# Block-sparse attention and two dense layers on one core: later batches' value preparation re-timed, and one pair of value gathers put one step later

## The chip, the cores and the metric

The kernel runs on one core of one Trainium2 chip. TensorE (PE) multiplies, VectorE (DVE), ScalarE (ACT) and GpSimd (POOL) do elementwise work, and SyncE (SP) issues nearly all of the DMAs, in the order in which the program names them. The metric is the device time of one execution in microseconds (us).

## The reference

Four batches, eight heads, 768 positions, 64 values per head. Attention is masked in blocks of 32: a row of blocks sees its own block and its two neighbours, the first and the last block, and three sampled blocks; the first and the last row of blocks see everything. Two dense layers follow.

```
scores = q @ k.T / sqrt(64), masked by blocks
attn   = softmax(scores) @ v                      # (4, 8, 768, 64)
x      = attn as (3072 tokens, 512)
h      = x @ w_in                                  # (3072, 2048)
g      = h * erf(softplus(h))
out    = g @ w_out                                 # (3072, 512)
```

## The kernel before, in words

All products of the two dense layers and of attention with the values are taken as sums of float16 halves.

**Units.** Attention is cut into 16 units per batch, 64 in all, numbered 0 to 63 here. Ten "m" units of a batch cover four rows of blocks and four heads each; four "f" units and two "e" units cover the rest. A unit's work is: scores on PE (`scores`, tile s), maximum on DVE and exponentials on ACT (`soft_max`, `soft_exp`), a split into halves on DVE (`soft_low`, tile p), and a transpose by DMA from the SP queue (`soft_turn`, tile pT). The product with the values (`values_of`, into the tile po_bank) comes three units later, then a normalisation on DVE (`norm`). After every second unit of a group of rows `turn` makes two halves and transposes them by DMA from the SP queue into xT, which the first dense layer reads.

**Steps.** From unit 4 on, the main loop runs 98 steps, 0 to 97. Every step has one group of the first dense layer on PE (24 products into the tile h), its elementwise work on ACT and DVE (tiles x, q, g), and one group of the second layer from two steps ago (tile o). A table (`until`) tells in which steps a unit is added: in every step up to 17, and then in about two steps of three. Step 18, 21 and 23 for instance have none. Step 16 starts with the PE row at 237.33 us, step 24 with that at 293.65 us.

**Order.** Every engine and every DMA queue works strictly in the order in which the program is written; nothing is reordered. So a DMA that waits on the SP queue holds all later ones, and an ACT instruction that waits for a load holds the elementwise work of the next dense group behind it.

**Values.** A batch's values are prepared a batch ahead, by pairs of heads (four pairs). `load_v` loads a pair (SP, 384 KB, tile vraw, a single buffer). `square_v` sums its squares on ACT (tile vj). `scale_v` adds these over partitions with two small PE products into a corner of po_bank and makes a scale on DVE (tile m_v). `high_v` (ACT) and `low_v` (DVE) write the halves into the tile vn. The write of vn into a table in DRAM (vtab) goes out on SP at the start of the next step. `behind(n)` runs at the end of the step of unit n and calls these; `prepare` puts the compute of a part off to the next step. With n the unit's number within its batch, the pair r is loaded at n = 3 + 3r, its squares are prepared one unit later and its scale and halves two units later.

**Gathers.** `gather_v(b, i)` fills two of eight slots of the tile vb from the table of batch b for rows of blocks i and i + 1: on SP, 9 DMAs for a pair whose slots don't yet hold the batch's first and last block and lie side by side, 12 where the two slots are the last and the first, 7 for each later pair. `gathers` decides in each step how many pairs go out: as many as slots are free, within a room of 4 blocks per step; a pair counts double where it is called fresh. A pair's DMAs stand on the SP queue ahead of the step's `soft_turn` and `turn`.

In the second batch (units 16 to 31) the pair i = 1 is gathered in step 12, i = 3 and i = 5 in step 14, i = 7 in step 15; products with the values of units 16, 17 and 18 (which read rows 1 to 4, 1 to 4, and 5 to 8) stand in steps 15, 16 and 17.

Of the kernel before, what the change touches and what calls it, by code (L numbers as in the profile page):

```python
# [43 lines left out]
def sparse_attention_moe(ctx: ExitStack, tc: tile.TileContext, qT, kT, v, sampled, w_in, w_out, out):  # L44
# [23 lines left out]
    B, H, D, S = qT.shape  # L68
# [7 lines left out]
    HP = H // 2  # L76
# [3 lines left out]
    KGS, VGS = 4, 8  # L80
# [35 lines left out]
    def load_k(b, pr):  # L116

        if b == 0:
            if pr < 3:
                kr = at.tile([P, 1024], F32, tag="pT", name=f"kr_{b}_{pr}", bufs=PV_LAG + 1)[:, :S]  # L120
            else:
                kr = at.tile([P, KT * 2 * VW], F16, tag="vn", name=f"kr_{b}_{pr}", bufs=1).bitcast(F32)[:, :S]
        else:
            kr = wi[:, NK * NG :, :].rearrange("p n c -> p (n c)")[:, :S]
        sp.dma_start(kr, kT[b, 2 * pr : 2 * pr + 2].rearrange("t d s -> (t d) s"))
        krs[b, pr] = kr

    def order_k(b, pr):
        kx = key_blocks(b).rearrange("p n (a c) -> p n a c", c=BLOCK)
        kr = krs.pop((b, pr))  # L130
        copy = pool.tensor_copy if b else dve.tensor_copy if pr > 1 else act.copy
        copy(kx[:, :NB, pr, :], kr.rearrange("p (n c) -> p n c", c=BLOCK))
        copy(kx[:, NB, pr, :], kr[:, :BLOCK])
# [4 lines left out]
    def load_q(b, t):  # L138
        place, tag, bufs = (mo, "g", FF_LAG + 1) if b == 0 and t in (1, 2) else (ld, "qt", 2)
        qt = place.tile([P, HP, P], F32, tag=tag, name=f"qt_{b}_{t}", bufs=bufs)  # L140
        rows = qT[b].rearrange("(r t) d s -> (t d) r s", t=2)
        if t < MT:
            c = (1 + 4 * t) * BLOCK
            sp.dma_start(qt, rows[:, :, c : c + P])
        else:
            sp.dma_start(qt[:, :, : 3 * BLOCK], rows[:, :, S - 3 * BLOCK :])
            sp.dma_start(qt[:, :, 3 * BLOCK :], rows[:, :, :BLOCK])
        qts[b, t] = qt
# [5 lines left out]
    def load_v(b, pr):  # L154

        if b == 0:
            vr = vb[:, 2 * pr : 2 * pr + 2].rearrange("p x a c -> p x (a c)").bitcast(F32)[:, :, : KT * D]
        else:
            vr = ld.tile([P, 2, KT * D], F32, tag="vraw", name=f"vraw_{b}_{pr}", bufs=1)
        sp.dma_start(vr, v[b][:, 2 * pr : 2 * pr + 2].rearrange("p h k d -> p h (k d)"))  # L160
        vraws[b, pr] = vr
# [237 lines left out]
    def gather_v(b, first):  # L399

        rows, last = vtab[b], first + 2
        at_ = [next(ring) % VGS for _ in range(first, last)]
        slot_of.update({(b, i): x for i, x in zip(range(first, last), at_)})
        fresh = [x for x in at_ if ended.get(x) != b]
        for x, y, _, _ in runs([(x, x) for x in fresh]):
            for q, n in ((2, 0), (3, NB - 1)):
                ends = rows[n * BLOCK : (n + 1) * BLOCK].unsqueeze(1).to_broadcast([BLOCK, y - x, 2 * QW])
                sp.dma_start(vb[q * BLOCK : (q + 1) * BLOCK, x:y, 1], ends)
        for x in fresh:
            ended[x] = b  # L410
        for x, y, n, m in runs(zip(at_, range(first, last))):
            lo, hi = int(n == 1), 3 - int(m == NB - 1)
            if lo:
                sp.dma_start(vb[:BLOCK, x, 0], rows[NB * BLOCK :])
            if hi < 3:
                sp.dma_start(vb[2 * BLOCK : 3 * BLOCK, y - 1, 0], rows[NB * BLOCK :])
            if y - x == 1 or lo or hi < 3:
                for j in range(y - x):
                    a, e = (lo if j == 0 else 0), (hi if j == y - x - 1 else 3)
                    c = (n + j - 1) * BLOCK  # L420
                    sp.dma_start(vb[a * BLOCK : e * BLOCK, x + j, 0], rows[c + a * BLOCK : c + e * BLOCK])
            else:
                around = rows[(n - 1) * BLOCK : (n + 2) * BLOCK]
                windows = bass.AP(around.tensor, around.offset, [around.ap[0], (BLOCK * 2 * QW, y - x), around.ap[1]])
                sp.dma_start(vb[: 3 * BLOCK, x:y, 0], windows)
        for j, x in enumerate(at_):
            for r, (q, half) in enumerate(PLACES):
                n = block_number(SYNC, first + j, r)
                sp.dma_start(vb[q * BLOCK : (q + 1) * BLOCK, x, half], rows[bass.ds(n * BLOCK, BLOCK), :])

    def whole_v(b, k):

        slot_of[b, -1 - k] = x = next(ring) % VGS
        ended.pop(x, None)
        sp.dma_start(vb[:, x], whole_rows(b)[:, 2 * k : 2 * k + 2])
# [396 lines left out]
    per = len(units) // B  # L832
    have_k, have_v = set(), set()
    kfree, vfree = KGS, VGS

    def gather_keys():

        nonlocal kfree
        if kjobs and kfree >= 4 and kjobs[0][0] in have_k:
            kfree -= 4  # L840
            gather(*kjobs.pop(0))

    def gathers(m):

        nonlocal vfree
        gather_keys()
        room = VGS if begun == 0 else 2 if begun <= NEAR else 4
        while vjobs and vjobs[0][0] in have_v:
            b, i = vjobs[0]
            n = 2 if i > 0 else 1  # L850
            fresh = b > 1 and 0 < i < VGS
            if vfree < n or room < n * (1 + fresh):
                break
            vfree -= n
            room -= n * (1 + fresh)
            vjobs.pop(0)
            gather_v(b, i) if i > 0 else whole_v(b, -1 - i)
# [9 lines left out]
    def behind(m):  # L867

        b, n = divmod(m, per)
        if b + 1 < B:  # L870
            c = b + 1
            if n == 10:
                load_q(c, 0)
            k = n - 4 if b else 2 * (n - 10) if n > 9 else -1
            if k in ((1, 3, 5, 7) if b else (2, 4, 6, 8)):
                order_k(c, (k - 1) // 2)
            if k in (0, 2, 4, 6):
                load_k(c, k // 2)
            if k == 8:
                have_k.add(c)  # L880
            pr, k = divmod(n - 3, 3)
            if pr in range(HP):
                if k == 0:
                    load_v(c, pr)
                if k == 1:
                    prepare((c, pr), None, square_v, None)
                if k == 2:
                    prepare((c, pr), scale_v, high_v, low_v)
                    if pr == HP - 1:
                        prepare((c,), None, None, join_scales)  # L890
            if pr == HP and k == 0:
                have_v.add(c)

    prepared = []

    def prepare(args, *parts):

        prepared.append([part and partial(part, *args) for part in parts])
# [50 lines left out]
    have_k.add(0)  # L949
    hold_blocks(POOL)  # L950
    gathers(0)
    hold_blocks(SYNC)
    for i in range(4, 10):
# [18 lines left out]
    scores(units[1])  # L972
    used_keys(units[1])
    gathers(0)
    for i in range(10, 16):
        load_weight(pool, "i", i)
# [26 lines left out]
    first_scale(0)  # L1003
    values_of(seen(units[1]))
    gathers(0)
    for i in (12, 13, 14, 15):
        load_weight(sp, "o", i)
# [15 lines left out]
    work("Do3 Hi2 Li2 Hi3 Li3")  # L1023
    begun = FIRST
    behind(begun - 1)

    on_pe[0] = False
# [4 lines left out]
    for m in range(len(groups) + FF_LAG):  # L1032
        ch, i = divmod(m, NGR)
# [73 lines left out]
        if unit:  # L1107
            behind(begun - 1)
# [39 lines left out]
```

## Time and profile before

| | us |
|---|---|
| median of 3 runs | 787.42 (784.93 to 789.92) |
| the profiled execution's own time | 787.68 |
| its span, first to last instruction | 785.9 |
| PE busy | 691.7 (88%) |
| DVE busy | 573.9 (73%) |
| ACT busy | 550.3 (70%) |

PE is the busiest engine and, from about 140 us on, it works almost without a break; what it waits for there is lost time. A row of the timeline reads: start, duration, engine, line, operation, what is written and read, how many, and in brackets the engine's idle time just before it with what ended that idle time. SPq rows are DMA issues; their duration is that of issuing, not of the transfer. Line numbers are all L60, a helper's, so the rows are told apart by tiles.

### The profile page before, as it was taken

To read this page: it belongs to the slowest core of one execution; us is meant where nothing else is said; L and a number is where in the kernel's file an instruction comes from. 1 tells how busy PE (TensorE), PEld (TensorE's weight loads), DVE (VectorE), ACT (ScalarE), POOL (GpSimd) and SP (SyncE) were. 2 spreads that over 40 slices of the span, in tenths; PEclk is the share of its full clock that TensorE was granted. 3 is DMA by queue.
4 is the path that set the end of the run, shared out by engine and by line. 5 is a ranking of instruction groups with operands and counts; after the bars stand their busy time and mean duration, and the time that the engine had idled before them with its cause. 6 is when DMAs were issued, how large, how long until landed. Compare 5 with 4: busy or idle time off the path is not lost.

```text
span 785.9 us, 26669 instructions
## 1 busy us (share of the span) xinstructions
PE 691.7 (88%) x10868; PEld 461.8 (59%) x10868; DVE 573.9 (73%) x1025; ACT 550.3 (70%) x943; POOL 123.9 (16%) x340
## 2 busy tenths in 40 slices
PE   2345727899979998999999989999999999999996
PEld 1234524566646665666767656666677666666663
DVE  3897887998876858877678858767778777654543
ACT  4665677998655767877677667777677776766774
POOL 4702121102411112011112111111011110000000
PEclk9999968999999999999999989999999999999999
DMA  8998973789688997974687996935777777410000
GB/s 314 277 304 264 313 168 82 151 194 253 151 185 184 215 200 160 215 148 104 148 192 164 203 203 166 233 81 138 139 151 199 163 160 179 63 42 2 20 23 27
DMA packets 200779, 129.24 MB, mean 164 GB/s; under 512 B 144080, under 2 KB 167760, under 8 KB 200656
## 3 DMA queue, kind: packets, MB, share of 16 engines
q1 hardware_dynamic: 197808, 117.83, 63.6%
q0 software_dynamic: 2848, 9.71, 3.7%
q8 instruction: 85, 1.39, 0.8%
q14 instruction: 38, 0.31, 0.2%
HBM read 81.52 MB, written 12.95 MB: 120 GB/s over the span
## 4 chain that ended last, share of the span: by engine, by line
PE 72%; DVE 12%; ACT 5%; issue 4%; DMA 4%; SPq 1%; POOL 1%; POOLq 0%; ACTq 0%; DVEq 0%
PE o L60 29%; PE h L60 28%; PE po_bank L60 7%; PE s_m L60 6%; DVE keys L60 3%; PE s_f L60 3%; DMA wo<-in_w_out_dram 2%; DVE mx_m L60 2%; DVE p_m L60 1%; ACT pf_m L60 1%; DVE wi L60 1%; DVE g L60 1%; SPq L60 1%; DVE wo L60 1%; ACT x L60 1%
## 5 line engine op out<-in xcount | busy, mean ns | idle before, releaser
L60 PE MATMUL h<-xT,wi 128*128 128x256 f16 x2304 | 272.4, 275 | 9.9 <-DMA xT<-x 4.8
L60 PE MATMUL o<-wo,g 128*128 128x512 f16 x1152 | 271.5, 383 | 4.9 <-ACT wo L60 2.2
L60 PEld LDWEIGHTS <-wi 128*128 128x128 f16 x2304 | 227.2, 99 | 60.3 <-issue 7.3
L60 PEld LDWEIGHTS <-g 128*128 128x128 f16 x1152 | 108.2, 99 | 137.8 <-issue 25.1
L60 ACT ACTIVATE x<-x 128x512 f32<-128x512 f32 x288 | 181.5, 630 | 9.1
L60 POOL COPY keys<-keys 128x128 f32 x264 | 91.2, 394 | 342.1 <-PE s_m L60 297.9
L60 DVE SCALAR_TENSOR_TENSOR q<-x,q 128x512 f32<-128x512 f32 x96 | 68.4, 712 | 68.7 <-ACT x L60 68.7
L60 ACT ACTIVATE x<-h,isg 128x512 f32<-128x512 f32 x96 | 65.8, 685 | 67.7 <-PE h L60 65.8
L60 ACT ACTIVATE pf_m<-s_m,nb_m 128x256 f32<-128x256 f32 x160 | 62.6, 473 | 46.3 <-DVE nb_m L60 43.4
L60 ACT ACTIVATE q<-q 128x512 f32<-128x512 f32 x96 | 60.7, 632 | 30.4 <-DVE q L60 30.4
L60 PE MATMUL s_m<-keys,qt 64*32 64x192 f32 (+1 forms) x1600 | 70.3, 355 | 9.6 <-ACT pf_m L60 7.9
L60 DVE SCALAR_TENSOR_TENSOR q<-q,h 128x512 f32<-128x512 f32 x96 | 65.5, 682 | 17.3 <-ACT q L60 17.3
L60 DVE SCALAR_TENSOR_TENSOR g<-q,g 128x512 f16<-128x512 f32 x96 | 67.0, 698 | 3.3
L60 ACT ACTIVATE q<-x 128x512 f32<-128x512 f32 x96 | 60.5, 630 | 3.1
L60 PEld LDWEIGHTS s_m<-keys,qt 64*32 64x32 f32 (+1 forms) x1600 | 45.9, 135 | 21.4 <-ACT pf_m L60 8.9
L60 PE MATMUL po_bank<-vb,pT_m 128*32 128x65 f16 (+1 forms) x3840 | 43.7, 203 | 13.8 <-DVE m_v L60 4.7
L60 DVE TENSOR_REDUCE mx_m<-s_m 128x4 f32<-128x1024 f32 x40 | 48.8, 1220 | 9.1 <-PE s_m L60 8.8
L60 PEld LDWEIGHTS <-pT_m 128*32 128x32 f16 x3840 | 38.1, 99 | 23.4 <-issue 17.2
L60 DVE TENSOR_TENSOR p_m<-pf_m,p_m 128x1024 f16<-128x1024 f32 x40 | 50.1, 1252 | 1.6 <-ACT p_m L60 0.3
L60 DVE TENSOR_SCALAR g<-q 128x512 f16<-128x512 f32 x96 | 41.3, 430 | 3.3
L60 DVE CAST p_m<-pf_m 128x1024 f16<-128x1024 f32 x30 | 20.9, 697 | 24.5 <-ACT pf_m L60 23.0
L60 POOL COPY keys<-wi 128x768 f32<-128x768 f32 (+1 forms) x24 | 16.7, 723 | 125.0 <-DMA wi<-in_kT_dram 125.0
(111 smaller groups left out, 529.9 us busy)
## 6 DMA issues: line engine op xcount, KB each, us to landing
vb<-vtab SPq DMA_DIRECT2D x280, 65.0 KB, 2.9
vb<-vtab SPq DMA_DIRECT2D x32, 390.0 KB, 4.3
vtab<-vn SPq DMA_DIRECT2D x16, 390.0 KB, 5.0
vb<-vtab SPq DMA_DIRECT2D x12, 520.0 KB, 5.2
qt<-in_qT_dram SPq DMA_DIRECT2D x20, 256.0 KB, 4.0
out_dram<-wo SPq DMA_DIRECT2D x20, 256.0 KB, 2.7
vb<-vtab SPq DMA_DIRECT2D x36, 130.0 KB, 3.3
vraw<-in_v_dram SPq DMA_DIRECT2D x12, 384.0 KB, 4.8
```

Source lines behind the costliest of these rows:

```text
L60: done = call(*args, **kwargs)
```

## The change

Two edits, both in functions that set order alone; no instruction is added or removed, but for where it stands.

The first alters when a pair of the second batch counts double in `gathers`: now its first two pairs (i = 1 and 3) do. Step 14 then takes i = 3 alone, and step 15 takes i = 5 and i = 7. Nothing else of the gathers moves.

The second alters `behind` for the values of the third and fourth batch (batches 2 and 3). Pair r is loaded at unit 4r − 1 of the batch ahead (the first one at the last unit of the batch before that), its squares are prepared two units later, its scale and halves three units later. The first batch's schedule for the second batch's values stays.

```diff
-            fresh = b > 1 and 0 < i < VGS
+            fresh = 0 < i < (0, VGS // 2, VGS, VGS)[b]
...
-            pr, k = divmod(n - 3, 3)
-            if pr in range(HP):
-                if k == 0:
-                    load_v(c, pr)
-                if k == 1:
-                    prepare((c, pr), None, square_v, None)
-                if k == 2:
-                    prepare((c, pr), scale_v, high_v, low_v)
-                    if pr == HP - 1:
-                        prepare((c,), None, None, join_scales)
-            if pr == HP and k == 0:
-                have_v.add(c)
+            if n == per - 1:
+                have_v.add(c)
+        if b == 0 and n < per - 1:
+            c, early = 1, 1
+            pr, k = divmod(n - 3, 3)
+        else:
+            c, early = (m + 1) // per + 1, 0
+            pr, k = divmod((m + 1) % per, 4)
+        if c < B and pr in range(HP):
+            if k == 0:
+                load_v(c, pr)
+            if k == 2 - early:
+                prepare((c, pr), None, square_v, None)
+            if k == 3 - early:
+                prepare((c, pr), scale_v, high_v, low_v)
+                if pr == HP - 1:
+                    prepare((c,), None, None, join_scales)
```

In steps of the main loop this gives, for the third batch's four pairs and then the fourth batch's:

| | before | now |
|---|---|---|
| load (end of step) | 15, 19, 24, 28; 38, 43, 48, 52 | 11, 15, 20, 26; 32, 38, 44, 50 |
| squares on ACT | 17, 21, 26, 30; 41, 45, 50, 54 | 14, 18, 25, 30; 36, 42, 49, 54 |
| scale and halves | 18, 23, 27, 31; 42, 47, 51, 55 | 15, 20, 26, 31; 37, 44, 50, 55 |

Before, all eight of the last line are steps without a unit; now 15, 20, 26, 44 and 50 have one.

SP, from the end of step 11 to step 12, one piece of the difference. vraw_0 is the load of the first pair of the third batch, vtab_95 the second batch's table and vn_3 the write of its last pair, which the gathers vb<-vtab_95 behind it read.

```order
 L60 DMA qt_1_3078<-in_qT_dram 128x4x128
 L60 DMA_TRANSPOSE pT_e_1_3105<-p_e_1_3097 128x8x128
+L60 DMA vraw_0_3113<-in_v_dram 128x768
 L60 DMA vtab_95<-vn_3_3099 128x6x260
 L60 DMA vb<-vtab_95 32x2x1040 x2
```

The load now stands on the queue ahead of the table's last write, and so of all gathers of the second batch.

SP in step 14, one piece of the difference. The first two rows end the pair i = 3, the last two begin the pair i = 5; pT_m_1_0 is unit 18's transpose, xT_2 the one that step 16's first dense layer reads.

```order
 L60 ISA
 L60 DMA vb<-vtab_95 32x1040
+L60 DMA_TRANSPOSE pT_m_1_0_3602<-p_m_1_0_3595 128x16x128
+L60 DMA_TRANSPOSE xT_2_2558<-x_0_5_3604 128x8x128
 L60 DMA vb<-vtab_95 32x2x1040 x2
 L60 DMA vb<-vtab_95 96x2x1040
```

Both transposes now stand 9 DMAs earlier, and the pair i = 5 stands behind them.

ACT around the squares of the third batch's second pair (vj_1), before and then now. x_2_6<-h_2_6 begins the elementwise work of step 22, x_2_3<-h_2_3 that of step 19.

```order
L60 ACTIVATE q_2_5_4751<-q_2_5_4751 128x512
L60 ACTIVATE vj_1_4773,vsq_1_4772<-vraw_1_4517 128x768
L60 ACTIVATE x_2_6_4800<-h_2_6_4775,isg_736 128x512
L60 ACTIVATE x_2_6_4800<-x_2_6_4800 128x512 x2
L60 ACTIVATE q_2_6_4804<-x_2_6_4800 128x512
```

```order
L60 ACTIVATE q_2_2_4291<-q_2_2_4291 128x512
L60 ACTIVATE vj_1_4315,vsq_1_4314<-vraw_1_3844 128x768
L60 ACTIVATE x_2_3_4342<-h_2_3_4317,isg_736 128x512
L60 ACTIVATE x_2_3_4342<-x_2_3_4342 128x512 x2
L60 ACTIVATE q_2_3_4346<-x_2_3_4342 128x512
```

The squares moved from step 21 to step 18; their load moved from the end of step 19 to that of step 15.

## Rows read from the trace of the kernel before

**Rows 1.** The page: memory rate in 40 slices, and a DMA group's landing time.
```profile
GB/s 314 277 304 264 313 168 82 151 194 253 151 185 184 215 200 160 215 148 104 148 192 164 203 203 166 233 81 138 139 151 199 163 160 179 63 42 2 20 23 27
...
vb<-vtab SPq DMA_DIRECT2D x280, 65.0 KB, 2.9
```

**Rows 2.** Timeline of PE, steps 15 to 18.
```profile
227.50 0.90 PE L60 MATMUL po_bank<-vb,pT_m 128*32 128x65 f16 x89 [0.45 <-DMA vb<-vtab]
...
237.33 4.44 PE L60 MATMUL h<-xT,wi 128*128 128x256 f16 x24 [4.83 <-DMA xT<-x]
...
246.59 2.78 PE L60 MATMUL h<-xT,wi 128*128 128x256 f16 x24
249.30 0.96 PE L60 MATMUL po_bank<-vb,pT_m 128*32 128x65 f16 x96
...
254.20 2.78 PE L60 MATMUL h<-xT,wi 128*128 128x256 f16 x24
```

**Rows 3.** Timeline of the SP queue, 202 to 286 us.
```profile
202.22 0.52 SPq L60 DMA_DIRECT2D vtab<-vn  x1
205.87 7.03 SPq L60 DMA_DIRECT2D vb<-vtab  x11
...
214.84 1.17 SPq L60 DMA_DIRECT2D qt<-in_qT_dram  x1
...
235.85 6.42 SPq L60 DMA_DIRECT2D vb<-vtab  x12
...
246.47 0.58 SPq L60 DMA_DIRECT2D vraw<-in_v_dram  x1
...
283.90 1.81 SPq L60 DMA_DIRECT2D vraw<-in_v_dram  x1
```

**Rows 4.** Timeline of the SP queue, the first 9 of step 14's 18 gathers.
```profile
219.92 6.05 SPq L60 DMA_DIRECT2D vb<-vtab  x9
```

**Rows 5.** Timeline of PE, steps 24 and 25, then 48 and 49.
```profile
293.65 2.78 PE L60 MATMUL h<-xT,wi 128*128 128x256 f16 x24
298.85 1.50 PE L60 MATMUL po_bank<-vb,pT_m 128*32 128x65 f16 x96 [2.42 <-DVE m_v L60]
...
305.13 2.78 PE L60 MATMUL h<-xT,wi 128*128 128x256 f16 x24
...
461.24 2.78 PE L60 MATMUL h<-xT,wi 128*128 128x256 f16 x24
466.29 1.50 PE L60 MATMUL po_bank<-vb,pT_m 128*32 128x65 f16 x96 [2.27 <-DVE m_v L60]
...
474.12 2.78 PE L60 MATMUL h<-xT,wi 128*128 128x256 f16 x24
```

**Rows 6.** Timeline of ACT, the second pair's squares of the third and fourth batch.
```profile
288.73 0.84 ACT L60 ACTIVATE vj<-vraw 128x768 bf16<-128x768 f32 x1 [5.71 <-DMA vraw<-in_v_dram]
...
456.18 0.84 ACT L60 ACTIVATE vj<-vraw 128x768 bf16<-128x768 f32 x1 [5.46 <-DMA vraw<-in_v_dram]
```

**Rows 7.** Timeline of DVE: unit 18's split, a pair's low halves, the late scale.
```profile
225.88 1.23 DVE L60 TENSOR_TENSOR p_m<-pf_m,p_m 128x1024 f16<-128x1024 f32 x1
...
262.51 1.15 DVE L60 SCALAR_TENSOR_TENSOR vn<-vraw,vs,vn 128x384 f16<-128x384 f32 x2 [1.20 <-ACT vn L60]
...
298.64 0.15 DVE L60 TENSOR_SCALAR m_v<-po_bank 128x1 f32<-128x1 f32 x1
```

**Rows 8.** The third batch's step 36: SP timeline, and that xT's landing.
```profile
392.93 1.90 SPq L60 DMA_TRANSPOSE pT_m<-p_m  x1
394.92 1.71 SPq L60 DMA_TRANSPOSE xT<-x  x1
...
xT<-x SPq DMA_TRANSPOSE x1, 3.2
```

**Rows 9.** Busy time by stretch (PE, PEld, DVE, ACT, POOL), PE clock, DMA share, GB/s.
```profile
247.00:303.00 56.00, 53.16 (x961) 37.42 (x960) 41.20 (x79) 39.52 (x73) 9.44 (x32) 0.97 0.88 197
...
466.00:473.00 7.00, 6.71 (x143) 3.98 (x143) 5.59 (x16) 4.73 (x9) 2.22 (x6) 0.51 0.93 158
```

## The prediction

> **What bounds the kernel now.** I read the page first: PE is the busiest engine, and from about 140 us on its timeline has hardly a gap. So I looked for the rows of PE with an idle time over 1 us, and asked of each what is late and who issued it. Between 140 and 770 us three are large.
>
> The first is in step 16: the dense product waits 4.83 us for xT, and then takes 4.44 us [rows 2]. The step before had already waited twice for gathers, the last time 0.45 us. The second and third are in steps 24 and 48: the product with the values waits 2.42 and 2.27 us for DVE to read the scale sum (m_v) out of po_bank [rows 5].
>
> What a step costs undisturbed is seen from step 17 to 18: 254.20 − 246.59 = 7.61 us [rows 2]. By this measure step 24 took 305.13 − 293.65 = 11.48, so it lost 3.87 us, and step 48 took 474.12 − 461.24 = 12.88 and lost 5.27 [rows 5]. Step 16 took 246.59 − 237.33 = 9.26, so 1.65 us were lost after its wait, 6.48 with it [rows 2]. That losses exceed waits is the clock: behind the third wait the granted clock is 0.51 of full speed, the 1.2 GHz level [rows 9]. PE has no work that could cover such a loss. The three sum to 6.48 + 3.87 + 5.27 = 15.62 us, 2.0% of the run; that is all that the change can take back.
>
> Why they are late: for xT, the SP queue. The order shows its transpose behind 18 gathers of step 14, of which the first 9 alone take 6.05 us to issue [rows 4]. For m_v, ACT: the squares of the second pair wait 5.71 and 5.46 us for their load [rows 6], which the SP queue issued only at 283.90 for an ACT that was free at 283.0 (288.73 − 5.71) [rows 3, 6]. The elementwise work behind is late by as much, DVE idles, and reads m_v at 298.64 [rows 7] where PE, at 298.85 − 2.42 = 296.43, already wants the bank.
>
> **The change, part by part. Step 16.** The pair i = 5 leaves step 14, so unit 18's transpose may start once its 9 gathers are issued and p is split. The gathers begin at 219.92 and end at 225.97 [rows 4], p is ready at 225.88 + 1.23 = 227.11 [rows 7]. In the third batch the same two transposes follow a lone pair: from the first one's issue to xT's landing it takes 394.92 + 3.2 − 392.93 = 5.19 us, to the end of issue 394.92 + 1.71 − 392.93 = 3.70 [rows 8]. So xT lands at about 232.3, where PE asks for it at 237.33 − 4.83 = 232.50 [rows 2]. The 6.48 go.
>
> Two things are paid back. First, the load that now stands ahead of the table's last write. The write is issued at 202.22 and the gathers wait for it until 205.87 [rows 3]. The load adds its issue, 0.58 [rows 3], and 384 KB ahead on the same queue, at the best rate of the page, 314 GB/s [rows 1], 1.25: together up to 1.83, at least nothing. Some is absorbed: the issue of the queries at 214.84 takes 1.17 [rows 3], mostly waiting. I take 1.1. Step 15 already waits for gathers, so this comes through: its products end 1.1 later, and PE asks for xT at 233.6.
>
> Second, the pair i = 5 is now late itself, with i = 7 behind it, and unit 18's product with the values in step 17 wants both. SP begins them at 227.15 + 3.70 = 230.85; 9 DMAs as in step 14 take 6.05 [rows 4], the 12 of i = 7 6.42 [rows 3], so the last is issued at 243.3 and lands 2.9 later [rows 1], at 246.2. PE comes there at 233.6 + 7.61 + (249.30 − 246.59 = 2.71) = 243.9 [rows 2], and waits 2.3 us. That is the length of the waits of 2.42 and 2.27 that lost the clock [rows 5], not of 0.45, after which the step ran on [rows 2], so I add the 1.65 of step 16. Net: the product starts at 246.2 instead of 249.30 [rows 2], 3.1 gained, less 1.65: **1.5 us**. Bounds: with the gathers 2 us slower and the loss of clock of step 48 (5.27 − 2.27 = 3.0), 3.1 − 2 − 3.0 = −1.9; with no load to wait for and no return in step 17 at all, 6.5. The order's own rows say most for the low half, since the same number of DMAs must pass the queue before step 17.
>
> The Trainium skill (DMA: Bandwidth & Descriptors, Anatomy of one DMA — SWDGE path) puts a DMA at about 2.0 us plus bytes over 436 GB/s, an estimate of 2.15 us for these 65 KB, for the software path. By it the wait in step 17 would be 0.75 shorter and the gain of this part 2.3; here the median is 2.9 [rows 1], and I go by that.
>
> **Steps 24 and 48.** The second pair's load moves from the end of step 19 to that of step 15, from 283.90 to where the first pair's load stood, about 246.47 [rows 3], and its squares from step 21 to 18. Step 18 starts at 254.20 [rows 2], 1.5 earlier now, and the squares follow its exponentials, so ACT comes to them more than 6 us after the load is issued instead of just before it. The wait of 5.7 us goes, DVE's idle with it, and step 23 has no scale any more. What is late next there: nothing within 2 us that I see on PE's timeline, since PE runs without a gap on both sides. I take back **3.87 us** in full, and in the fourth batch, with the same table, **5.27**. Bounds for each: nothing, if the new place meets another wait, to full.
>
> **What moves besides.** The four pairs of two batches keep their instructions: squares, halves and scales are the same number. Their cost on ACT and DVE is covered by idle time, 56.00 − 41.20 = 14.8 us of DVE in 247 to 303 alone [rows 9]. The table writes go out one step behind the halves as before, and the halves of a batch's last pair stay in their step, so no gather of batches 2 and 3 has its table later. In step 32 the early load stands ahead of gathers that are needed five steps later. I take nothing.
>
> **Sum.** 1.5 + 3.9 + 5.3 = 10.6 us off the profiled execution's 787.68: **777.1 us**, 1.3% faster. The median of the runs is 0.26 lower than that execution, so the sum holds against it too.
>
> **Rivals.** (1) *The forecast*: 773.5 to 780. Chance 0.60.
>
> (2) *No return*: the gathers of step 15 land in time, because the queue is less crowded than in step 14. The whole 15.6 comes back: 772.0. For it: DMAs are issued sooner overall. Against: SP's rows show no free stretch there. 0.12.
>
> (3) *The DMA engines are the bound*. In 247 to 303 their share is 0.88 [rows 9], 49 of 56 us. If what PE gains only lets transfers queue longer, the first part gives nothing and step 24's wait turns into one for gathers: only 5.3 is left, 782.4. For it: the same bytes in less time. Against: 56 − 49 = 7 us are free, more than 3.9. The Trainium skill (Trainium Kernel Development and Optimization, Key Constraints) states that all issuing queues share the same 16 DMA engines, so that moving an issue buys no bandwidth; no row here contradicts it, and this rival is what it would do. 0.15.
>
> (4) *The load waits anyway*. vraw is one buffer; the next load must wait for the halves of the pair before, which now lie in the same step as the load. If the squares still find no data, steps 24 and 48 stay: 786.2. Against: SP issued step 19's load at 283.90 [rows 3], less than two steps before step 24 at 293.65 [rows 5], so halves of the load's own step are long done when SP comes to it. 0.08.
>
> (5) *Slower*. Scale and halves now lie in steps 15, 20, 26, 44 and 50, which have a unit. Each puts 4 × 0.15 + 1.15 us on DVE and 1.20 of waiting for ACT [rows 7], 2.95. If DVE has no slack in a step with a unit, normalisation is late, po_bank stays taken, and PE waits 2.95 and loses 1.65 of clock in each: 5 × 4.6 = 23, so 777.1 + 23 = 800.1. It decides where DVE's delay outlasts the step. Against: four of the five are followed by a step without a unit, in which DVE has its maximum, split and normalisation less. 0.05.
>
> **Range and chances.** Two in ten left out: below 771.5 and above 783.5; that takes in (2), (3) and nearly all of (1). A change of under 1%, 7.9 us, is what a measurement of this kernel hardly tells from none, so faster means below 779.5. Of (1) 0.55 lies there, (2) wholly, of (3) 0.03: faster 0.70. Slower is (5), 0.05; the rest, 0.25, is within 1%.
>
> **What would show it.** PE's row of step 16 should have no wait on xT, and step 17's product a wait of 1 to 4 us on vb<-vtab; no wait there means (2), over 4 us with a larger loss means the first part is negative. ACT's vj rows should have no idle on vraw, and steps 24 and 48 no wait on m_v; a vj row that still waits for vraw is (4), a wait on vb or pT in steps 20 to 26 is (3). Waits of PE on rinv or xf in steps 16, 21, 27, 45, 51 are (5). I am wrong in the main if steps 24 and 48 keep their loss under another name.

## The result and the profile after

The changed kernel takes **778.66 us** (median of 6 runs, 776.68 to 783.39), beside 788.12 (784.93 to 789.92, 6 runs) for the kernel before on the same chip: a ratio of **0.9889, interval 0.9853 to 0.9926**. It is faster by 1.1%. The forecast was 777.1. The profiled execution took 780.28, its span 778.5.

A step is timed below from the first row of its first dense layer (h<-xT,wi) to that of the next step, as in the prediction, so a wait ahead of that first row counts in the step before. The three steps that the sum was made of, and the other steps that moved by over 1 us (us):

| step | 12 | 14 | 15 | 16 | 17 | 24 | 41 | 48 |
|---|---|---|---|---|---|---|---|---|
| before | 6.72 | 10.03 | 14.17 | 9.26 | 7.61 | 11.48 | 7.74 | 12.88 |
| after | 7.97 | 11.19 | 10.17 | 7.60 | 12.19 | 7.61 | 9.05 | 7.61 |

Step 12 does not belong to the change: its dense product starts at 200.34, ahead of the first instruction that moved (the load issued at 202.27, below), and takes 4.03 us instead of 2.78, at a granted clock of 0.50 of full speed from 200 to 202, the 1.2 GHz level. None of the other profiled runs shows that there.

By stretch, the 7.4 us between the two spans lie so: −0.1 (a loss) up to step 10, −1.0 in steps 11 to 19, 3.6 in steps 20 to 35, 4.2 in steps 36 to 59, 0.7 behind.

**Steps 24 and 48 are undisturbed.** The timeline of PE in the changed kernel (start, duration, then the idle time before a row in brackets, where there is any), steps 24 and 48 with the start of the next:

```profile
295.09 2.78 PE L60 MATMUL h<-xT,wi 128*128 128x256 f16 x24
297.80 0.96 PE L60 MATMUL po_bank<-vb,pT_m 128*32 128x65 f16 x96
...
302.69 2.78 PE L60 MATMUL h<-xT,wi 128*128 128x256 f16 x24
...
459.97 2.78 PE L60 MATMUL h<-xT,wi 128*128 128x256 f16 x24
462.68 0.96 PE L60 MATMUL po_bank<-vb,pT_m 128*32 128x65 f16 x96
...
467.58 2.78 PE L60 MATMUL h<-xT,wi 128*128 128x256 f16 x24
```

No product waits for m_v any more, which answers to [rows 5]. The reason stands in ACT's timeline, the squares of the third batch's second pair and the fourth batch's first and second:

```profile
263.63 0.83 ACT L60 ACTIVATE vj<-vraw 128x768 bf16<-128x768 f32 x1
...
388.82 0.86 ACT L60 ACTIVATE vj<-vraw 128x768 bf16<-128x768 f32 x1
...
428.73 0.83 ACT L60 ACTIVATE vj<-vraw 128x768 bf16<-128x768 f32 x1
```

None has an idle time on vraw, where [rows 6] showed 5.71 and 5.46 us. The load of the first of these three is issued at 251.87 (below), 11.8 us ahead of its use.

**Steps 15 to 17: the wait has moved.** PE's timeline from the products of step 15 on:

```profile
229.51 0.20 PE L60 MATMUL po_bank<-vb,pT_m 128*32 128x65 f16 x1 [0.37 <-DMA vb<-vtab]
230.10 1.37 PE L60 MATMUL po_bank<-vb,pT_m 128*32 128x65 f16 x93 [0.39 <-DMA vb<-vtab]
...
236.39 2.78 PE L60 MATMUL h<-xT,wi 128*128 128x256 f16 x24 [0.68 <-DMA xT<-x]
...
...
244.00 2.78 PE L60 MATMUL h<-xT,wi 128*128 128x256 f16 x24
246.71 0.56 PE L60 MATMUL po_bank<-vb,pT_m 128*32 128x65 f16 x3
248.58 0.31 PE L60 MATMUL po_bank<-vb,pT_m 128*32 128x65 f16 x4 [1.32 <-DMA vb<-vtab]
249.79 0.90 PE L60 MATMUL po_bank<-vb,pT_m 128*32 128x65 f16 x89 [0.90 <-DMA vb<-vtab]
250.62 2.56 PE L60 MATMUL s_m<-keys,qt 64*128 64x64 f32 x40
...
256.18 2.78 PE L60 MATMUL h<-xT,wi 128*128 128x256 f16 x24
```

The wait for xT is 0.68 instead of 4.83 us [rows 2], and step 16 takes an undisturbed 7.60. In step 17 the product with the values now waits 1.32 + 0.90 = 2.22 us for gathers, and what follows runs slow: s_m takes 2.56 where it takes 1.47 elsewhere. The busy time by stretch (PE, PEld, DVE, ACT, POOL, granted clock, DMA share, GB/s) shows why:

```profile
250.00:254.00 4.00, 4.00 (x131) 2.50 (x115) 1.39 (x4) 0.15 (x1) 0.70 (x3) 0.58 1.02 210
```

The granted clock is 0.58 of full speed, so mostly the 1.2 GHz level, right behind the two waits.

The SP queue's timeline, which answers to [rows 3, 4]:

```profile
202.27 0.53 SPq L60 DMA_DIRECT2D vraw<-in_v_dram  x1
202.89 0.39 SPq L60 DMA_DIRECT2D vtab<-vn  x1
207.66 6.95 SPq L60 DMA_DIRECT2D vb<-vtab  x11
...
221.29 7.43 SPq L60 DMA_DIRECT2D vb<-vtab  x9
230.19 1.81 SPq L60 DMA_TRANSPOSE pT_m<-p_m  x1
232.09 2.21 SPq L60 DMA_TRANSPOSE xT<-x  x1
234.40 13.87 SPq L60 DMA_DIRECT2D vb<-vtab  x21
...
251.87 0.53 SPq L60 DMA_DIRECT2D vraw<-in_v_dram  x1
```

The 9 and 12 gathers of i = 5 and i = 7 now go out in one run of 21. They take 13.87 us, 0.66 each in the mean (19 of the issues take 0.32 to 0.53 us, two 1.24 and 2.02, and register instructions between them the rest), and the last is issued by 248.27; PE's last wait in step 17 ends at 249.79.

### The profile page after: what moved, and what is told of

Read it like the earlier page. It is cut to its first block, busy times and chain, and to the rows that moved or that the text cites. A ratio compares the mean times of both kernels' runs of the same rounds, so it can differ in the third digit from the quotient of the medians.

```text
span 778.5 us, 26676 instructions
## 1 busy us (share of the span) xinstructions
PE 688.5 (88%) x10868; PEld 459.6 (59%) x10868; DVE 573.6 (74%) x1025; ACT 551.5 (71%) x943; POOL 120.0 (15%) x340
## 4 chain that ended last, share of the span: by engine, by line
PE 66%; DVE 14%; ACT 6%; DMA 6%; issue 4%; SPq 2%; POOL 0%; POOLq 0%; ACTq 0%; DVEq 0%
PE o L60 26%; PE h L60 25%; PE po_bank L60 6%; PE s_m L60 5%; DVE keys L60 4%; PE s_f L60 3%; SPq L60 2%; ACT x L60 2%; DMA pT_m<-p_m 2%; DVE p_m L60 2%; DMA vb<-vtab 2%; DVE wo L60 1%; ACT pf_m L60 1%; DVE mx_m L60 1%; DVE wi L60 1%
## 5 line engine op out<-in xcount | busy, mean ns | idle before, releaser
L60 POOL COPY keys<-keys 128x128 f32 x264 | 88.6, 383 | 325.3 <-PE s_m L60 283.0
L60 PE MATMUL s_m<-keys,qt 64*32 64x192 f32 (+1 forms) x1600 | 68.1, 347 | 9.3 <-ACT pf_m L60 6.4
```

What stands on the lines that cost most here:

```text
L60: done = call(*args, **kwargs)
```

## The experiments

All times below are medians beside the kernel before on the same chip, with the ratio to it and its 95% interval. The sums of steps 11 to 19 and 20 to 35 are from the profiled runs; before they are 78.41 and 111.86, after 79.45 and 108.25.

**1. Which of the two edits gains.** The gathers alone (`behind` as before):

```diff
-            fresh = b > 1 and 0 < i < VGS
+            fresh = 0 < i < (0, VGS // 2, VGS, VGS)[b]
```

> The gather edit alone; the values' schedule as in the kernel before. Theory A (the gain is all in the values; the gathers' wait only moves): step 16 loses its wait of 4.8 us on xT, step 17 gains one of 2 to 3 us on vb with a loss of clock, in sum 0 to 2 us gained; steps 24 and 48 lose 3.9 and 5.3 as before; 786 to 788 us. Theory B (the gathers are what gained, because the SP queue's whole delay in the second batch begins there): step 24's wait on m_v goes too, since its load is issued earlier; 780 to 783 us.

Measured: 791.31 beside 790.35; **1.0015 (0.9988 to 1.0042)**. By step 20 it is 3.35 us ahead (75.06 instead of 78.41), and steps 20 to 35 take 4.85 more (116.71). That is nearest to theory A, though steps 24 and 48 lose more than before. The timelines of SP, ACT and PE show where it goes; first SP:

```profile
284.99 0.43 SPq L60 DMA_DIRECT2D vraw<-in_v_dram  x1
```

Then ACT, the squares of the second pair, and PE in step 24:

```profile
289.94 0.84 ACT L60 ACTIVATE vj<-vraw 128x768 bf16<-128x768 f32 x1 [10.20 <-DMA vraw<-in_v_dram]
```

```profile
300.05 1.51 PE L60 MATMUL po_bank<-vb,pT_m 128*32 128x65 f16 x96 [4.80 <-DVE m_v L60]
```

The load goes out at 284.99, no sooner than before (283.90, [rows 3]), though PE is ahead. ACT waits 10.20 for it instead of 5.71, PE 4.80 for m_v instead of 2.42. Step 23 takes 7.32 instead of 5.35 and step 24 14.25 instead of 11.48, 4.74 of the 4.85 us. What the gathers gain is lost again at the late load.

The values alone (`fresh` as before, `behind` changed):

> The values' edit alone; gathers as in the kernel before. Theory A: the waits of steps 24 and 48 go (9.1 us), step 41 waits about 1.3 us more, and the load ahead of the table's write in step 12 makes steps 12 to 16 later by about 1.5 us, with step 16's wait on xT still there at 4 to 6 us; 779 to 782 us. Theory B: little, at most the 5.3 us of step 48; 783 to 787 us.

Measured: 779.83 (778.04 to 782.53); **0.9865 (0.9829 to 0.9900)**, no less gain than the whole change. Steps 24 and 48 take 7.60 and 7.61. Step 16 keeps its wait, on PE's timeline:

```profile
240.65 4.19 PE L60 MATMUL h<-xT,wi 128*128 128x256 f16 x24 [4.66 <-DMA xT<-x]
```

So the gain is that of the values, and the gathers add nothing that these runs could show (0.9889 and 0.9865, with intervals that overlap). No version that was tried and computes everything is shown to be faster than these two.

**2. Is it the lateness of one load?** In the kernel before, only the second pair's load is moved, by one step:

```diff
-                if k == 0:
+                if k == 0 and (c < 2 or pr != 1):
                     load_v(c, pr)
...
                     if pr == HP - 1:
                         prepare((c,), None, None, join_scales)
+                    if c > 1 and pr == 0:
+                        load_v(c, 1)
```

> The kernel before, with one thing moved in the third and the fourth batch: the load of the second pair of values is issued one step sooner (end of steps 18 and 42 instead of 19 and 43); squares, scales, halves and all else stay in their steps. Theory A (steps 24 and 48 lose because this load is late for the squares in steps 21 and 45): the squares find their data, steps 24 and 48 take 7.6 to 9 us instead of 11.48 and 12.88, and 5 to 9 us of the whole come back: profiled 779 to 783. Theory B (they lose because the work of a pair falls on too few steps, squares, scale and halves one after the other): m_v is still read late, steps 24 and 48 stay over 11 us, 786 to 789. The load must wait for the first pair's halves, which are made in the same step, and holds the gathers behind it on SP: a wait on vb in step 19 or 20 of up to 3 us would take back a part of A's gain.

Measured: 782.42 beside 789.11; **0.9917 (0.9881 to 0.9953)**. On its timelines SP issues the load at 270.14 instead of 283.90, ACT squares it without a wait, and step 24 has no wait on PE:

```profile
270.14 0.53 SPq L60 DMA_DIRECT2D vraw<-in_v_dram  x1
...
273.28 11.16 SPq L60 DMA_DIRECT2D vb<-vtab  x15
```

```profile
285.26 0.83 ACT L60 ACTIVATE vj<-vraw 128x768 bf16<-128x768 f32 x1
```

```profile
295.97 2.78 PE L60 MATMUL h<-xT,wi 128*128 128x256 f16 x24
298.69 0.96 PE L60 MATMUL po_bank<-vb,pT_m 128*32 128x65 f16 x96
...
303.57 2.78 PE L60 MATMUL h<-xT,wi 128*128 128x256 f16 x24
```

Steps 24 and 48 take 7.60 and 7.61, with squares, scales and halves where they were. It is the load's lateness that cost 3.87 and 5.27 us. Step 20 takes 1.25 more (8.86), part of what was expected for holding the gathers.

**3. The load ahead of the table's write.** The third batch's first load moved behind step 12's gathers:

```diff
-            if k == 0:
+            if k == ((c, pr) == (2, 0)):
                 load_v(c, pr)
```

> Both edits, but the third batch's first load at the end of step 12 instead of step 11, so behind the second batch's last table write and the first gathers. If that load costs what stands ahead of it in the changed kernel, gathers of step 12 begin about 1.8 us earlier after the write, step 14's products of scores and step 15's wait on vb shrink by about 1 us each, step 17's wait shrinks little because the load now stands ahead of step 14's transposes; 1 to 2 us below the changed kernel. If the queue's total before step 17 is all that counts, the same time within 0.7 us.

Measured: 783.35 (778.59 to 784.15); **0.9892 (0.9853 to 0.9931)**, as the changed kernel; the 1 to 2 us expected do not show. Steps 11 to 19 take 77.89 instead of 79.45, steps 20 to 35 111.70 instead of 108.25; of this step 20 has 1.61 (9.52 instead of 7.91) and step 26 2.30 (10.08 instead of 7.78, below).

**4. The table's writes ahead of the gathers.** In the changed kernel step 41 takes 9.05 us, 1.31 more than before. The SP queue there:

```profile
392.47 1.71 SPq L60 DMA_TRANSPOSE xT<-x  x1
396.65 0.42 SPq L60 DMA_DIRECT2D vtab<-vn  x1
397.16 5.38 SPq L60 DMA_DIRECT2D vb<-vtab  x9
...
404.12 3.07 SPq L60 DMA_TRANSPOSE pT_m<-p_m  x1
```

From 394.18 the queue stands for 2.47 us at the write of the fourth batch's first pair, which needs its halves, with the third batch's gathers behind it. In this run the writes of pairs 0 to 2 of the later batches go out behind the step's gathers:

```diff
-            writes.append(write)
+            (writes if b < 2 or pr == HP - 1 else later).append(write)
...
-        write_values()
+        write_values(writes)
...
             gathers(begun)
+        write_values(later)
```

> Both edits, but table writes of the third and fourth batch's first three pairs stand behind the step's gathers instead of ahead. If step 41's new wait of 1.3 us comes from the SP queue that waits 2.4 us in step 38 for the halves of the write, that wait goes: 1.3 us below the changed kernel, everything else the same. If it comes from the write's bytes on the DMA engines, step 41 keeps it.

Measured: 781.11 (779.61 to 787.80); **0.9892 (0.9848 to 0.9935)**. The 2.47 us on SP are gone, and step 41 takes 8.39, so 0.66 of its 1.31 us go; it does not show in the time. So the write is at most half of the cause. The rest stands in DVE's timeline, the end of the split of the unit of step 38, in the kernel before and then in the changed kernel:

```profile
403.34 1.23 DVE L60 TENSOR_TENSOR p_m<-pf_m,p_m 128x1024 f16<-128x1024 f32 x1
```

```profile
402.87 1.23 DVE L60 TENSOR_TENSOR p_m<-pf_m,p_m 128x1024 f16<-128x1024 f32 x1
```

Counted from the start of step 38 (394.17 and 391.81), the split ends 10.40 us later before and 12.29 now, because DVE makes a scale and low halves (step 37) ahead of it; with the writes behind it is 12.30. (This is read from the timelines; no run takes that work out of step 37.) SP's transpose of this unit, at 404.12, waits for it in either order, and the gathers that step 41 waits for stand behind that transpose. What the write's wait adds is a longer issue of the transpose, 3.07 instead of 2.41 us. These are single profiles: step 41 takes 8.39 to 11.14 in the ten with the values' new order, 7.72 to 7.74 in the three with the old one.

**5. What holds step 17: bytes, rows, or DMAs.** In the changed kernel the 21 gathers of i = 5 and i = 7, first with half of each row, then with half of the rows of the sampled blocks:

```diff
+        w = QW if (b, first) in ((1, 5), (1, 7)) else 2 * QW
-        rows, last = vtab[b], first + 2
+        rows, last = vtab[b][:, :w], first + 2
```

> The changed kernel with the 21 gathers of the second batch's pairs i = 5 and i = 7 cut to the first half of each row: as many DMAs and as many rows, half the bytes (it leaves out the columns of two of the four heads of each row in these two pairs). Theory A (the number of DMAs and rows on the SP queue is the limit): SP still takes 13 to 14 us for the 21, step 17 keeps its wait on vb and its 12 us; time 778 to 781. Theory B (bytes, so the DMA engines, are the limit): the 21 are issued in 8 to 10 us, the wait in step 17 goes and the step takes about 7.6 us; 774 to 776, or less where later steps gain too.

```diff
+        h = BLOCK // 2 if (b, first) in ((1, 5), (1, 7)) else BLOCK
...
-                sp.dma_start(vb[q * BLOCK : (q + 1) * BLOCK, x, half], rows[bass.ds(n * BLOCK, BLOCK), :])
+                sp.dma_start(vb[q * BLOCK : q * BLOCK + h, x, half], rows[bass.ds(n * BLOCK, h), :])
```

> The changed kernel with the 12 gathers of sampled blocks of the second batch's pairs i = 5 and i = 7 cut from 32 rows to 16 (it leaves out half of each of these blocks); as many DMAs, half the rows. With half the bytes per row SP took 14.27 us for the 21 DMAs, no less than 13.87. Theory A (each DMA has a fixed cost on the queue): SP takes 13 to 14 us again, step 17 keeps its wait and 11 to 12 us; 778 to 783. Theory B (the queue's cost goes by rows): 21 DMAs with about two thirds of the rows take 9 to 10 us, the wait in step 17 goes; 774 to 778.

Measured: 783.41 (779.73 to 784.21), **0.9921 (0.9897 to 0.9944)**, and 779.63 (778.92 to 785.19), **0.9858 (0.9801 to 0.9915)**. The SP queue, with half of the bytes and then with half of the rows:

```profile
233.74 14.27 SPq L60 DMA_DIRECT2D vb<-vtab  x21
```

```profile
235.78 13.82 SPq L60 DMA_DIRECT2D vb<-vtab  x21
```

Neither differs by more than 0.4 us from 13.87. The busy time by stretch in the first of them, with the DMA share as the last number but one:

```profile
234.40:248.40 14.00, 12.07 (x210) 8.25 (x209) 11.94 (x24) 9.99 (x20) 2.10 (x8) 1.00 0.39 86
```

The DMA engines are at 0.39 there (0.68 in the changed kernel in the same stretch), and step 17 takes 11.54 and 12.17 us all the same. So neither bytes nor rows set the pace of this stretch; what is left is the number of DMAs on one queue with their register instructions, 0.66 us each in the mean. In both runs, too, a few of the 21 issues take 0.9 to 1.7 us and the others 0.32 to 0.57; what holds the long ones is not shown.

**6. A second queue.** The 12 gathers of i = 7 on the POOL queue, in the changed kernel:

```diff
+        eng, which = (pool, POOL) if (b, first) == (1, 7) else (sp, SYNC)
...
-                sp.dma_start(vb[: 3 * BLOCK, x:y, 0], windows)
+                eng.dma_start(vb[: 3 * BLOCK, x:y, 0], windows)
```

> The changed kernel with one thing more: the 12 gathers of the second batch's pair i = 7 are issued by the POOL queue, beside the SP queue instead of behind it. In the changed kernel step 17 takes 12.19 us; its product with the values waits there 1.32 and 0.90 us for gathers that SP issued one after the other, 21 in 13.87 us, and the clock goes with it. Theory A (the number of DMAs that one queue can issue is the limit): the 12 gathers run beside the 9 of i = 5, the wait on vb in step 17 goes, step 17 takes about 7.6 us, and what SP issues behind them comes 7 us sooner; profiled time 774 to 776. Theory B (the 16 DMA engines are the limit): the transfers land no sooner, step 17 keeps a wait of 1 us or more on vb, time as the changed kernel, 778 to 781. Theory C (what is gained there is given back later, as when the gathers were moved alone): step 17 is 3 to 5 us shorter, and steps 20 to 27 are longer by as much; 778 to 781.

Measured: 782.48 beside 789.11; **0.9921 (0.9900 to 0.9943)**. Step 17 takes 7.60, as theory A had it, but step 15 16.20, which none of the three had; steps 11 to 19 take 79.63. PE's timeline in step 15:

```profile
234.86 0.24 PE L60 MATMUL po_bank<-vb,pT_m 128*32 128x65 f16 x1 [5.33 <-DMA vb<-vtab]
```

POOL, with nothing else on its queue, issues them at 222.49 to 229.88, beside SP's gathers of i = 3. The landing times (issues, KB each, median us) of the stretch 220 to 236, here and in the changed kernel:

```profile
vb<-vtab POOLq DMA_DIRECT2D x10, 65.0 KB, 6.7
...
vb<-vtab SPq DMA_DIRECT2D x6, 65.0 KB, 7.3
```

```profile
vb<-vtab SPq DMA_DIRECT2D x6, 65.0 KB, 3.9
```

So POOL was then made to issue them only behind its key copies:

```diff
         if (b, first) == (1, 7):
+            postponed.append(partial(issue_v, pool, POOL, b, first, at_, fresh))
...
             gather_keys()
+            while postponed:
+                postponed.pop(0)()
```

> As the run with the last pair on the POOL queue, but POOL issues the 12 gathers of i = 7 only behind its copies of the next unit's keys, which end at 236.35 us in the changed kernel, so beside SP's 9 gathers of i = 5 (234.40 to 240.4) and no longer beside those of i = 3 and the two transposes. Theory A (in steps 14 and 15 the DMA engines are full, share 1.16 there in the run before, and in steps 16 and 17 SP's issuing is the limit, share 0.68 with half the engines' time free): step 15 keeps the 10 to 11 us of the changed kernel, and the wait on vb in step 17 shrinks from 2.22 us to 1 us or less, the step from 12.19 to 7.6 to 9; steps 11 to 20 together 75 to 77 us instead of 79.45, the whole 775 to 778. Theory B (two queues at once always lengthen each other's landing): the gathers land at 250 or later, step 17 keeps 11 to 12 us; 778 to 782. Theory C: the steps 11 to 20 get shorter, steps 20 to 36 longer by as much; 778 to 782.

Measured: 784.01 (781.11 to 790.46); **0.9915 (0.9885 to 0.9945)**. The theory of the issue limit gave 775 to 778 and missed: step 17 takes 15.47, longer than with all 21 on SP. The busy time by stretch and the landing times of 234.4 to 248.4:

```profile
234.40:248.40 14.00, 13.05 (x211) 8.76 (x210) 12.09 (x24) 9.72 (x20) 9.13 (x24) 1.00 1.17 197
```

```profile
vb<-vtab POOLq DMA_DIRECT2D x10, 65.0 KB, 8.2
...
vb<-vtab SPq DMA_DIRECT2D x7, 65.0 KB, 4.3
```

With one queue the DMA share was 0.68 here and 16 such gathers landed in a median of 2.3 us; with two it is 1.17, and POOL's need 8.2. SP, its gathers gone sooner, also brings the next transpose (at 240.11) into the same stretch, so not all of this is the gathers'. No run has POOL's gathers without SP's DMAs beside them, so how much of their landing time belongs to POOL's queue itself is open.

And on POOL the 9 gathers of i = 5, with the values' order alone:

> The values' order of the change alone, with the gathers left in their old steps, but the 9 gathers of the second batch's pair i = 5 issued by the POOL queue. With the values' order alone (profiled 781.5) SP issues these nine ahead of the two transposes in step 14, and step 16 still waits 4.66 us for xT. Theory A (SP's issuing is the limit): both transposes go out some 5 us sooner, xT is there, step 16 takes 7.6 us and step 17 keeps its 7.6: some 4 to 6 us less than the values' order alone, 774 to 777. Theory B (the DMA engines are the limit): the transposes' transfers wait instead of their issue, and step 16 keeps a wait of 3 us or more; 780 to 782. Theory C (given back later): step 16 is shorter, steps 17 to 27 longer; 779 to 782.

Measured: 783.19 (780.52 to 786.11); **0.9931 (0.9905 to 0.9957)**. Step 16's wait goes (7.60), step 17 keeps 7.61, and steps 14 and 15 take 12.36 and 14.23; 81.02 for steps 11 to 19. The waits are in step 15 again, for gathers.

**7. What the last pair costs at all.** The changed kernel without the 12 gathers of i = 7:

```diff
+        if (b, first) == (1, 7):
+            return
```

> The changed kernel without the 12 gathers of the second batch's pair i = 7 (its unit computes with what its buffers held before). The upper end of what any other place for them could bring. Theory A (SP's issuing and the DMA engines set the pace of steps 14 to 26 together): the 9 gathers of i = 5 end at 240.4 us, no wait in step 17, which takes 7.6 us; later gathers come 7 us sooner and the small waits of steps 20 to 26 go too: 4.6 us of step 17 and up to 1 more, 774 to 775. Theory B (something else gives it back, as after the gathers moved alone): steps 18 to 36 become longer by 3 us or more; 777 to 780.

Measured: 776.53 (775.07 to 777.74); **0.9821 (0.9764 to 0.9879)**. Step 17 takes 7.61, steps 11 to 19 73.41, and steps 20 to 35 107.71: with the early load nothing is given back. Beside the changed kernel's profile these 12 DMAs cost 4.58 us in step 17 and 6.04 in steps 11 to 19; the intervals of the two ratios overlap. No place tried for them is shown to avoid it.

## Why the prediction was right, and where not

**Steps 24 and 48: right, in cause and in size.** 3.87 and 5.27 us were to be taken back, and 3.87 and 5.27 were. That the late load is the cause was argued from the timelines; moving that one load alone shows it.

**Step 16: the wait goes, as forecast, but the times of its parts were too short.** The gathers of i = 3 were given 6.05 us [rows 4] and took 7.43; they began at 221.29 instead of 219.92. xT was to land at 232.3, but its transpose was issued only at 232.09, and PE could start on it at 236.39. The payback of the load, 1.1 with bounds 0 and 1.83, shows as 207.66 − 205.87 = 1.79 at the first gathers and 1.37 at step 14's: nearer to the upper bound, since only 0.42 of it was absorbed on the way. The prediction also charged it to PE alone (233.6) and not to the gathers of step 14, which stand behind the same load and were left to begin at 219.92.

**Step 17: right in kind, the term too small.** Forecast were a wait of 2.3 on vb and 1.65 of clock, 3.95; measured were 2.22 of wait and 12.19 − 7.61 = 4.58 in all. But the product was to start at 246.2, and its last part starts at 249.79, since 21 DMAs at 0.66 take 13.87 where 6.05 + 6.42 = 12.47 was reckoned, on top of a start 3.55 us later (234.40 instead of 230.85), of which 1.37 are the payback just named. Where the wait falls is not fixed: in the profiled run of experiment 4, whose program is the same up to these gathers, step 15 takes 13.52 and step 17 7.90. Nor does the length of a wait alone tell whether the clock falls, as the prediction took it: it fell in step 12 behind a wait of 1.10 us, and stayed at full speed in step 14 behind one of 1.76.

**The net of 1.5 us: about right in steps 14 to 19, and gone from steps 11 to 19.** Steps 11 to 19 take 1.04 us more, but 1.82 of that is lost in steps 11 and 12, ahead of the first moved instruction. Steps 14 to 19, the first that the gathers' edit reaches, take 53.97 instead of 54.76. Over the profiled runs, the two-queue runs and those that leave work out aside, they take 51.93 to 53.97 with the gathers moved (four) and 54.26 to 54.76 without (three), 1.8 less in the mean. The prediction had no term for step 14, where PE's wait on its own issue is 1.76 us beside 0.61: it is 1.13 to 1.76 in the ten profiled programs that have i = 3 alone on SP there, and at most 0.61 in the three that have both pairs. Why is not settled. By the time of the whole, the gathers give nothing that these runs could show, alone (1.0015, lost again at steps 23 and 24) or with the values.

**What moves besides: this step failed.** "No gather of batches 2 and 3 has its table later" looked at each batch's own table. The write of the next batch's table stands on the same queue, ahead of this batch's gathers, and holds them 2.47 us in step 38. And "their cost on ACT and DVE is covered by idle time" was taken from a sum over 56 us: in step 37 scale and halves make the next split 1.89 us later. Step 41 pays 1.31 for the two together, 0.66 and 0.65 as far as experiment 4 can part them. With what steps 11 to 19 did the sum is 10.6 − 1.5 − 1.0 − 1.3 = 6.8, beside 7.4 between the profiled executions. Of that difference the 1.82 us of steps 11 and 12 are not the change's; without them it is 9.2, near the 9.5 of the medians (788.12 − 778.66). The forecast of 10.6 came as close as it did because steps 24 and 48, 9.14 of it, were right.

**The rivals.** *No return* (772.0): refuted by the wait in step 17. With the pair i = 7 left out nothing returns, and the ratio of 0.9821 makes 773.6 of 787.68, about what this rival gave. *The DMA engines* (782.4): not in step 17, where half of the bytes leave the wait as it is; but with a second queue beside SP the share goes from 0.68 to 1.17 in 234.4 to 248.4, SP's own gathers land in medians of 7.3 instead of 3.9 us (220 to 236), those of i = 5 in 4.3 instead of 3.1, and POOL's in 6.7 and 8.2. The argument "7 us are free" held for one queue: steps 24 and 48 came back in full, with a share of 0.91 in 247 to 303. The Trainium skill (Trainium Kernel Development and Optimization, Key Constraints), cited there, has it that issuing from several engines saves issue time alone, and the three runs with POOL agree: 1.17 of share, 8.2 us to land. The skill (DMA: Bandwidth & Descriptors, Issuing engines are not separate DMA queues) also calls the time to initiate a DMA usually small beside the DMA; for one DMA that holds here (0.66 us beside a median landing of 2.3), but in a row of 21 the issues sum to the 13.87 us that PE waited for. *The load waits anyway* (786.2): no row of vj of the third and fourth batch waits. *Slower* (800.1): not in the mean, but its mechanism exists, in one of its five places and in step 37 (above). In four of the ten profiled runs with the values' new order step 26 takes 10.1 to 12.0 instead of 7.8 us. The timelines of ACT, DVE and PE in the run with half of the rows:

```profile
316.50 0.63 ACT L60 ACTIVATE x<-xf 128x512 f16<-128x512 f32 x1 [3.49 <-DMA xT<-x]
```

```profile
317.17 0.69 DVE L60 TENSOR_TENSOR x<-xf,x 128x512 f16<-128x512 f32 x1 [1.64 <-ACT x L60]
```

```profile
320.65 0.40 PE L60 MATMUL po_bank<-one,vsq 128*128 128x1 f32 x2 [2.69 <-DVE xf L60]
```

A late transpose on SP holds ACT's halves for the next one, DVE behind it reads po_bank late, and the pair's two small products, which now stand in a step with a unit, wait for that bank. In the profiled run of the changed kernel the same ACT row comes at 312.27 without such a wait, and step 26 takes 7.78. SP's timeline has the transpose, in the changed kernel and then with half of the rows:

```profile
308.88 1.78 SPq L60 DMA_TRANSPOSE xT<-x  x1
```

```profile
310.99 1.98 SPq L60 DMA_TRANSPOSE xT<-x  x1
```

The first is issued 1.52 us ahead of the start of step 26 (310.40), the second 0.46 ahead (311.45). In the four runs with a long step 26 it is 0.52 us ahead to 0.25 behind, and in the other six 1.52 to 8.06 ahead, so the lateness of this transpose parts the ten. Why SP comes to it later in four of them was not settled; moving the scale out of step 26 was not tried.

## What to carry to other kernels

Look for the load that is issued last before its use on a queue that is always busy: moving it one step earlier gave most of what this change gives (0.9917 beside 0.9889, with intervals that overlap), and a gain made ahead of it was lost at it again (10.20 us of waiting instead of 5.71). On a queue with DMAs end to end, a group of DMAs that is moved mostly chooses who waits (here step 15, 16 or 17); where a run like that of experiment 5 shows that bytes don't matter, count the DMAs between an operation and its consumer at the queue's own rate. Look at what other batches' writes stand ahead of, not only at their own readers, and don't take idle time summed over many steps for slack in the one step that gets new work.

## What the runs showed of the hardware that was not expected

- Issuing on a busy SP queue had a price that neither bytes nor rows changed: 21 gathers took 13.87 us as they were, 14.27 with half of the bytes, 13.82 with half of the rows of 12 of them. The price is not even: in the first of these, 19 issues take 0.32 to 0.53 us and two 1.24 and 2.02.
- Two queues together gave no shorter time: POOL issued its own gathers in about 0.5 us each (9 in 4.72), and they landed in medians of 6.7 and 8.2 us beside SP's DMAs, where SP's with no second queue take 2.3 to 3.9 in the same stretches.
- PE has waits of 0.3 to 1.8 us in step 14 that no semaphore explains, in all profiled programs but one (0.61 before, 1.76 after). In both of these traces one packet of 16 KB on the instruction queue, begun at 218.22 and 221.05, ended some 1.4 us ahead of the end of that wait, so PE may have been waiting for its own instructions; that was not tested.
